# A start-up section rewritten: block 0's masks as their own matmuls, and causal triangles on the tensor engine

## The chip, the core and the metric

One core of a Trainium2 chip runs the whole kernel. Its engines work at once, each from its own queue in order: TensorE (PE, with its weight loads PEld), VectorE (DVE), ScalarE (ACT), GpSimd (POOL, which also issues DMAs) and SyncE (SP, which here only issues DMAs). The metric is the device time of one execution in microseconds. A profile of one execution gives every instruction's start and duration and what ended each wait.

## The reference

Four batches, eight heads, 768 positions of 64 elements. The keys are cut into 24 chunks of 32. Each query takes the six chunks with the largest upper bound of its scores, attends to the causal positions in them, and the result goes through a feed-forward layer with softplus.

```python
k_min, k_max = k_chunks.min(axis=3), k_chunks.max(axis=3)      # per chunk and element
ub = sum(maximum(q * k_min, q * k_max), axis=-1)               # bound per query and chunk
ub = where(causal chunk, ub, -1e9); top = six largest chunks
scores = scale * q @ k.T, where selected and pos_q >= pos_k, else -1e9
attn = softmax(scores) @ v                                     # [4, 8, 768, 64]
x = attn as [3072, 512]
out = softplus(x @ w_in) @ w_out                               # w_in [512, 2048], w_out [2048, 512]
```

## The kernel before

The work is cut into 12 blocks of 256 query positions (three per batch, `NBLK`), and each block into four pairs of heads. A block's way is this.

- Its k and q are loaded and turned so that head elements lie on partitions: blocks 0 to 2 by PE transposes (`kT`, `qT`, L471), later ones by transposing DMAs on SP (L475). k and q of block 0 come as float32 over SP (`load_pairs`, tiles `xp`) and are cast on ACT or DVE (L258, L259); all other loads, the weights too, are issued by POOL (L339, L376, L383).
- DVE reduces k to chunk maxima and minima (`kx`, L490, L498), which are copied into `BD`. The positive and negative parts of q (`qpos`, `qneg`) against `BD` give the bounds (`ub`, L570, L574), from which DVE takes the sixth largest (L597) and writes the mask rows (`mraw`, L612, L615). They are turned (`mT`, L627, L633) and copied into the rows of `qa` and `qt` beside q.
- `ka` and `kb` hold k of a whole batch, one head of each pair in either, and beside it one-hot rows that name each position's chunk. One matmul (L687, L688) over the 96 or 128 rows so yields score and mask at once. The one-hot rows are made by POOL's affine selects in `ohb` (L275 to L279) and spread into `ka` and `kb` by SP (L307).
- ACT takes the exponential of the scores (L695). On the diagonal POOL clears the triangle above it, in place, by an affine select (L705): eight per block, between the exponential and the matmul with v.
- The matmul with v (`av`, L717) carries a column of ones for the sum; DVE divides (L727, L728); the result is turned into `x` (L743 and a copy, or a transposing DMA, L732).
- The feed-forward layer: `h` (L791, 96 tasks of eight matmuls), exp and ln on ACT (L796, L801), `y` (L816), a copy and a store per 128 rows (L827).

The order on every engine is laid out ahead: `make_plan` lists every operation with its engines, its estimated cost, the buffers it takes and a due time from the table `PAR`; `Plan.run` lays them out in time, for each engine the earliest due among those that can start, and the instructions are emitted in that order. `keep_awake` fills PE's planned gaps of the first part with matmuls of a tile of zeros (L852). `PAR` holds the due times (`a`, `prep`, `hlag`, ...), the times of loads (`first`, `loads`, `ahead`) and the number of buffers of each kind (`sizes`).

Of the kernel before, what the change touches and what calls it, by code (L numbers as in the profile page):

```python
# [12 lines left out]
ALU = mybir.AluOpType  # L13
# [50 lines left out]

class Op:
    __slots__ = ("name", "alts", "fn", "deps", "gate", "after", "succ", "alloc", "touch", "key",
                 "rel", "packet", "port", "due", "wait", "eng", "start", "end", "done", "dma", "n", "at", "inst")


class Plan:  # L70
# [5 lines left out]
    def op(self, name, alts, fn, deps=(), alloc=(), touch=(), key=None, dma=None, gate=(), after=(), rel=0.0, packet=19.0, port=False):  # L76
        o = Op()
        o.rel, o.packet, o.port = round(rel), packet, port
# [50 lines left out]
    @staticmethod  # L129
    def home_at(pool, s, e):  # L130
        t = 0.0
        for q, x, dma in pool.ends[s]:
            t = max(t, x + (LANDED[e] if dma else 0 if q == e == "PE" else LAT[q].get(e, 150)))
        return t

    def run(self, par):
# [11 lines left out]
        ring, packet = {"SP": 0.0, "POOL": 0.0}, {"SP": 19.0, "POOL": 32.0}  # L148
# [3 lines left out]
        while ready:  # L152
# [26 lines left out]
            if o.dma:  # L179
                other = "SP" if e == "POOL" else "POOL"  # L180
                at = max(o.end + (650 if e == "SP" else 1150), ring[e], 2650.0)
                back, part = max(0.0, ring[other] - at), packet[other] / o.packet
                ring[e] = at + o.dma + min(o.dma * part, back)
                ring[other] += min(o.dma, back / part)
                packet[e] = o.packet
                o.done = ring[e] + (450 if o.packet < 100 else 1000)
                if e == "SP":
                    o.end = max(o.end, ring[e] - 3500)
            else:
                o.done = o.end  # L190
# [4 lines left out]
            for b in o.touch:  # L195
                b.left -= 1
                b.ends.append((e, o.done, bool(o.dma)))
# [22 lines left out]
def dve(n, rate=1.0):  # L220
    return n / (0.96 * rate) + 66


PAR = dict(
    dmat=3,
    dmaT=450,
    narrow=1,
    l0=1,
    over="soy",
    maskD=3,  # L230
    awake=(1.06, 45.0, 5.7),
    first=(64.42, 64.23, 29.03, 95.39),
    loads=((87.43, 130.15, 71.7), 19.14, (76.86, 12.06, 15.17), 41.22),
    tol={"PE": 0, "ACT": 0, "DVE": 0, "POOL": 2358, "SP": 0},
    alt=636,
    ohd=(229.35, 150.58),
    a=(-46.8, -33.92, -31.03, -0.05, 17.1, 24.77, 54.71, 88.7, 133.12, 175.62, 173.66, 255.42, 297.45, 469.8),
    prep=((77.31, -48.97, -81.43, 46.38), (-8.14, 24.92, -67.86, -43.68), (53.78, -16.07, -58.0, 11.26), (25.03, -41.37, -16.45, 11.23)),
    av=(-0.8, 4.76),
    ot=(12.12, 10.86),  # L240
    hlag=(8.7, 27.7, 34.1, -3.53, 34.9, 33.84, 33.54, 32.2, 25.36, -32.32, 54.03, 77.81),
    ylag=(7.32, 7.87, 25.64, 26.35, 28.67, 47.05, 47.88, 49.45, 10.02, 22.03, 47.36, 37.39),
    ahead=(3.4, 19.67, 10.64, 22.05, 12.72, 9.33, 70.63, 47.4, 103.95),
    sizes=dict(s=2, h=2, y=1, o=1, t=2, xf=2, xp=4, kT=2, io=8, kx=2, q=2, pn=2, ub=2, pt=4, osb=4, x=4, g=2, e=4, ysb=4, mT=2),
# [3 lines left out]
def make_plan(T, par):  # L248
# [19 lines left out]
    P.op("zero", [("DVE", 80)], lambda e: nc.vector.memset(T.zero, 0.0), key=-100000)  # L268
    ident = P.op("ident", [("POOL", 520)], lambda e: make_identity(nc, T.ident), key=1000)
    ohm = P.op("ohm", [("DVE", 700)], lambda e: nc.vector.memset(T.ohb, NEG), key=900)  # L270
    oh = []
    for k in range(NBLK):
        def f(e, k=k):
            x = T.ohb[:, k * QB:(k + 1) * QB]
# [6 lines left out]
        oh.append(P.op("oh", [("POOL", 1330)], f, [ohm], key=1500 + 6000 * k))  # L281
# [13 lines left out]
    chunk_rows = [P.op("c4", [("POOL", 900)], f4, [r4], key=3000)]  # L295
    mr0, bd0, kb0, vone, ohk = [], [], [], [], {}
# [8 lines left out]
    def rows_of(i, k0, k1, h):  # L305
        x = (T.KB[i][32:64] if h else T.KA[i][64:96])[:, :, k0 * QB:k1 * QB]
        return nc.sync.dma_start(out=x, in_=T.ohb[:, k0 * QB:k1 * QB].unsqueeze(1).to_broadcast([32, NP, (k1 - k0) * QB]))  # L307
    for k0, k1 in ((0, 1), (1, NBLK)):
        for h in range(2):
            o = P.op("ohk", [("SP", 450)], lambda e, k0=k0, k1=k1, h=h: rows_of(0, k0, k1, h), oh[k0:k1],  # L310
                     key=par["ohd"][k0] * 1e3, dma=300 * (k1 - k0))
# [16 lines left out]
    def load(nm, n, when, gate=()):  # L328
# [6 lines left out]
        for t in range(NT):  # L335
# [4 lines left out]
                     gate=gate, key=key, rel=key - 2000 if n > 2 else 0.0, dma=950 if n < 3 else 2050, packet=32.0, **new)  # L340
            first = first or o
            ld[nm, n, t] = o

    def load_pairs(nm, n, when):
# [4 lines left out]
        for g in range(2):  # L349
# [4 lines left out]
                     key=1e3 * when[g], dma=950, packet=29.0, alloc=[st])  # L354
# [6 lines left out]
    def load_rows(nm, n, when):  # L361

        for t in range(NT):
            st = Buf(pool["xf"])
            d = P.op(f"ld {nm}{n}.{t}", [("SP", 560)], lambda e, t=t, st=st: nc.sync.dma_start(out=st.ap, in_=rows(nm, n, t)),
                     key=1e3 * (when + 0.3 * t), dma=1000, alloc=[st])
# [5 lines left out]
    def load_w_in(when):  # L372
        for c in range(4):
# [4 lines left out]
            w_in.append(P.op(f"w_in{c}", [("POOL", 800)], f, key=1e3 * (when + 0.4 * c), dma=2550, packet=173.0, after=w_in[-1:]))  # L378

    def load_w_out(when):  # L380
        for c in range(4):
# [4 lines left out]
            w_out.append(P.op(f"w_out{c}", [("POOL", 800)], f, key=1e3 * (when + 0.4 * c), dma=2550, packet=173.0,  # L386
# [5 lines left out]
    load_pairs("k", 0, (0.0, l0[0]))  # L392
    if par["l0"] < 2:
        load_pairs("q", 0, (l0[1], l0[2]))
    else:
        load("q", 0, l0[1])
# [4 lines left out]
    for nm, x in zip("kqv", l1):  # L401
        load(nm, 1, x)
# [545 lines left out]
```

## Time and profile before

| | us |
|---|---|
| Median of 3 runs (264.2 to 266.11) | 266.11 |
| The profiled execution, its own time | 266.59 |
| Its span | 264.8 |
| POOL busy in the span | 110.8 |
| DMA moved | 29.87 MB, mean 113 GB/s |

The span runs from the first to the last instruction of the profile. "Busy" is time in which an engine has an instruction under way. The 40-slice view shows the parts by engine, in tenths:

```profile
PE   8698999999999999999999999999999999999995
DVE  6589961019789667447634596584582164221012
ACT  3589999988687879999687992699997885999900
PEclk9799999999999999999999999999999999999999
```

A slice is 6.6 us. PE counts as busy in nearly all, ACT and DVE in the first third above all; `PEclk` is the granted clock of the tensor engine.

### The profile page before, as it was taken

The page shows a single profiled execution, that of the slowest core. Times are in us where ns is not written, and L with a number is a line of the kernel's source. Part 1 is how long each engine was busy: PE and PEld are TensorE (multiplying, and loading weights), DVE is VectorE, ACT ScalarE, POOL GpSimd, SP SyncE. Part 2 cuts the span into 40 slices and gives each one's busy share as a digit, 9 for nine tenths or more (in the row PEclk, how much of TensorE's full clock was granted, in tenths as well). Part 3 has the DMA queues.
Part 4 walks back from the last instruction along what each step waited for, and adds up shares of the span by engine and source line. Part 5 has one row for each costly group of instructions (what it writes and reads, how often), then busy time and mean ns, then how long its engine had stood idle before and what let it go on. Part 6 is the DMA issues. An engine that isn't in the chain of part 4 may idle for free.

```text
span 264.8 us, 7039 instructions
## 1 busy us (share of the span) xinstructions
PE 255.0 (96%) x2750; PEld 197.2 (74%) x2779; DVE 142.5 (54%) x500; ACT 211.0 (80%) x372; POOL 110.8 (42%) x193
## 2 busy tenths in 40 slices
PE   8698999999999999999999999999999999999995
PEld 8698898768775677788678864777888756887744
DVE  6589961019789667447634596584582164221012
ACT  3589999988687879999687992699997885999900
POOL 8927878798318520543990263401110211310000
PEclk9799999999999999999999999999999999999999
DMA  7996999999999984699699969624440123001022
GB/s 162 161 189 90 181 196 231 155 139 190 149 136 173 132 119 89 115 129 100 73 173 150 117 88 174 173 54 120 45 82 0 42 72 99 10 2 42 0 79 79
DMA packets 114719, 29.87 MB, mean 113 GB/s; under 512 B 104544, under 2 KB 111712, under 8 KB 114688
## 3 DMA queue, kind: packets, MB, share of 16 engines
q0 software_dynamic: 74944, 13.11, 66.5%
q1 hardware_dynamic: 39744, 16.33, 33.0%
q8 instruction: 21, 0.34, 0.6%
q14 instruction: 10, 0.08, 0.1%
HBM read 27.26 MB, written 6.29 MB: 127 GB/s over the span
## 4 chain that ended last, share of the span: by engine, by line
PE 86%; DMA 5%; DVE 3%; ACT 3%; issue 1%; POOL 0%; DVEq 0%; POOLq 0%
PE ph L791 30%; PE py L816 17%; PE pt L816 9%; PE po L717 7%; PE ps L687 5%; PE py L852 4%; PE ps L688 4%; DMA io<-in_k_dram 3%; DMA x<-osb 3%; PE pt L687 2%; PE pt L688 1%; PE pt L570 1%; ACT g L801 1%; PE ph L816 1%; ACT e L796 1%
## 5 line engine op out<-in xcount | busy, mean ns | idle before, releaser
L791 PE MATMUL ph<-x,w_in_sb 128*128 128x256 bf16 x768 | 91.8, 272 | 0.0
L705 POOL TENSOR_SCALAR_AFFINE_SELECT pt<-pt 128x256 bf16<-128x256 bf16 x96 | 39.5, 419 | 112.6 <-ACT pt L695 112.1
L791 PEld LDWEIGHTS <-w_in_sb 128*128 128x128 bf16 x768 | 73.6, 98 | 11.5 <-DMA w_in_sb<-in_moe_w_in_dram 0.5
L695 ACT ACTIVATE pt<-ps 128x512 bf16<-128x512 f32 (+1 forms) x134 | 69.9, 564 | 9.4 <-PE ps L688 8.8
L796 ACT ACTIVATE e<-ph 128x512 f32<-128x512 f32 x96 | 56.3, 606 | 12.5 <-PE ph L791 11.8
L816 PEld LDWEIGHTS <-g 128*128 128x128 bf16 x400 | 37.4, 98 | 31.4 <-ACT g L801 0.5
L816 PE MATMUL py<-w_out_sb,g 128*128 128x512 bf16 x231 | 57.8, 379 | 1.5 <-ACT ysb L258 0.2
L801 ACT ACTIVATE g<-e 128x1024 bf16<-128x1024 f32 x48 | 51.1, 1072 | 1.0
L695 ACT ACTIVATE pt<-pt 128x512 bf16<-128x512 f32 (+1 forms) x58 | 32.4, 584 | 0.6 <-PE pt L688 0.6
L717 PEld LDWEIGHTS <-pt 128*128 128x128 bf16 x672 | 26.8, 97 | 5.1 <-issue 0.6
L259 DVE COPY ysb<-py 128x512 f32<-128x512 f32 x12 | 8.3, 691 | 36.9 <-PE py L816 36.9
L717 PE MATMUL po<-v,pt 128*128 128x65 bf16 x610 | 26.4, 193 | 0.3 <-DVE osb L728 0.3
L816 PE MATMUL pt<-w_out_sb,g 128*128 128x512 bf16 x108 | 26.2, 379 | 0.2
L727 DVE RECIPROCAL rec<-po 128x4 f32<-128x4 f32 x43 | 7.6, 178 | 34.9 <-PE po L717 34.6
L490 DVE TENSOR_REDUCE kx<-kT 128x32 bf16<-128x1024 bf16 x18 | 21.0, 1209 | 8.9 <-DMA kT<-io 8.9
L852 PE MATMUL py<-zero 128*128 128x128 bf16 x243 | 22.7, 245 | 1.1 <-DVE zero L268 1.1
L339 POOL DMA_DIRECT2D v<-in_v_dram x24 | 21.6, 905 | 3.8 <-DMA io<-in_q_dram 1.5
L339 POOL DMA_DIRECT2D io<-in_k_dram x22 | 20.0, 910 | 5.7 <-DMA w_in_sb<-in_moe_w_in_dram 2.2
L339 POOL DMA_DIRECT2D io<-in_q_dram x22 | 19.9, 910 | 0.7 <-PE ph L791 0.6
L728 DVE TENSOR_TENSOR osb<-po,rec 128x256 bf16<-128x256 f32 x43 | 18.2, 424 | 2.7 <-DMA x<-osb 1.3
L852 PEld LDWEIGHTS <-zero 128*128 128x128 bf16 x243 | 18.3, 111 | 1.3 <-DVE zero L268 1.1
L687 PE MATMUL ps<-qa,ka 96*128 96x256 bf16 x71 | 18.3, 273 | 0.7 <-DVE qa L259 0.7
(99 smaller groups left out, 302.5 us busy)
## 6 DMA issues: line engine op xcount, KB each, us to landing
out_dram<-ysb SPq DMA_DIRECT2D x23, 256.0 KB, 2.4
v<-in_v_dram POOLq DMA_DIRECT2D x24, 128.0 KB, 7.6
io<-in_k_dram POOLq DMA_DIRECT2D x22, 128.0 KB, 7.2
io<-in_q_dram POOLq DMA_DIRECT2D x22, 128.0 KB, 7.1
w_out_sb<-in_moe_w_out_dram POOLq DMA_DIRECT2D x4, 512.0 KB, 8.0
w_in_sb<-in_moe_w_in_dram POOLq DMA_DIRECT2D x4, 512.0 KB, 9.6
xp<-in_k_dram SPq DMA_DIRECT2D x2, 256.0 KB, 3.2
xp<-in_q_dram SPq DMA_DIRECT2D x2, 256.0 KB, 6.3
```

The lines of the kernel that those rows point to most:

```text
L339: lambda e, t=t: nc.gpsimd.dma_start(out=into(nm, n, t), in_=rows(nm, n, t)),
L490: nc.vector.tensor_reduce(kx.ap[:, :, j].rearrange("d p (t c) -> d t p c", t=NT), kT.ap.rearrange("d p x -> d (p x)").rearrange("d (t p c ...
L687: nc.tensor.matmul(sp.ap[:, 0:QB], kk[0:nr, p, j * 128:(j + 1) * 128], qq, start=True, stop=True)
L695: lambda e, sp=sp, pt=pt, h=h, j=j, w=w: nc.scalar.activation(pt.ap[:, h, j:j + 2].rearrange("k j c -> k (j c)")[:, 0:w], sp.ap[:, 0:w], A ...
L705: nc.gpsimd.affine_select(out=d, in_=d, compare_op=ALU.is_ge, fill=0.0, base=0, channel_multiplier=-1, pattern=[[0, 2], [1, 128]])
L717: nc.tensor.matmul(o[:, u, h], pt.ap[:, h, j, c0:c0 + 128], T.V[i][:, j, 2 * p + h, :], start=(j == 0), stop=(j == t0 + u))
L728: nc.vector.tensor_tensor(osb.ap[0], o[:, :, :, 0:D], osb.ap[1].to_broadcast([128, NT, 2, D]), op=ALU.mult)
L791: nc.tensor.matmul(o[:, j], T.w_in[:, dt, ft * 128:(ft + 1) * 128], x.ap[:, dt], start=(dt == 0), stop=(dt == KDM - 1))
L796: lambda e, hb=hb, eb=eb, f2=f2: nc.scalar.activation(eb.ap[:, f2 * 512:(f2 + 1) * 512], hb.ap, ACT.Exp),
L801: lambda e, eb=eb, g=g, f4=f4: nc.scalar.activation(g.ap[:, f4 * 4:(f4 + 1) * 4].rearrange("f j c -> f (j c)"), eb.ap, ACT.Ln, bias=1.0),
L816: nc.tensor.matmul(yb.ap[:, 0:c1 - c0], g.ap[:, f, u * 128:(u + 1) * 128], T.w_out[:, f, c0:c1], start=(f == 0), stop=(f == KFF - 1))
L852: z.fn = lambda e: T.nc.tensor.matmul(T.pools["y"].homes[0][:, 0:128], T.zero, T.zero, start=True, stop=True)
```

## The change

Block 0 (`plain = n < 1`) no longer builds `qa` and `qt` rows with masks. Its k is copied once, for both heads of a pair, into a tile `K0`, its transposed masks once into `M0`, and each score is two matmuls into one bank: `K0` with q, and `ohb` with `M0`. For that `ohb` has a second copy of block 0's one-hot columns in partitions 32 to 63 (`ohc`, on DVE or ACT). `ka` and `kb` still get block 0's k, for blocks 1 and 2, by copies from `K0` (`ke`, on POOL or DVE). q is not copied into `qa`.

```diff
+            plain = n < 1
+            if plain:
+                kcs.append(P.op(f"kc{n}", [("ACT", act(L * QB)), ("DVE", ...)],
+                                lambda e, ...: copy(e, *in_turn(T.K0[:, pp], t_of(kT), pairs)), [x0, x1], touch=[kT]))
+                kab[n, gi] = kcs * 2
+                for h in range(2 if ps is groups[-1] else 0):
...
+                        f"ke{n}", [("POOL", 1150), ("DVE", 380)],
+                        lambda e, ...: copy(e, (T.KB if h else T.KA)[i][hs, :, cs], T.K0[hs]),
...
-            qac = P.op(f"qac{n}", ...
+            qac = None if plain else P.op(f"qac{n}", ...
...
+            if plain:
+                mask[n, gi, 0] = mask[n, gi, 1] = P.op(
+                    f"mc{n}", [("DVE", 345), ("ACT", 480)],
+                    lambda e, ...: copy(e, T.M0[:, pp], mT.ap.bitcast(BF16)[0:64, 0:L * QB]...), mt, touch=[mT])
-            for h in range(2):
+            for h in range(0 if plain else 2):
```

In blocks 0 and 1 (`tri = n < 2`) the causal triangle is added to the diagonal's scores by a third matmul, of the identity with a tile `tri` that holds `NEG` above the diagonal; POOL's selects L705 are there for blocks 2 to 11 only.

```diff
+                            parts = [(T.K0, q.ap[1], slice(h * 64, h * 64 + 64)), (T.ohb, T.M0, slice(h * 32, h * 32 + 32))]
+                            for c0, c1, t in ((0, QB, 0), (QB, w, 1)):
+                                for z, (kk, x, ss) in enumerate(parts):
+                                    jj = slice(c0 // 2, c0 // 2 + 128)
+                                    kk = kk[ss, p, jj] if z == 0 else kk[ss, jj]
+                                    nc.tensor.matmul(sp.ap[:, c0:c1], kk, x[ss, p, t * 128:QB], start=z == 0, stop=z == 1 and not tri)
+                                if tri:
+                                    nc.tensor.matmul(sp.ap[:, c0:c0 + 128], T.ident, T.tri, start=False, stop=True)
+                            return
...
-                    if last:
+                    if last and not tri:
                         def f_a(e, pt=pt, h=h, t0=t0):
...
+        tri_ = [P.op("tri", [("POOL", 430)], lambda e: nc.gpsimd.affine_select(
+            out=T.tri, in_=T.tri, compare_op=ALU.is_ge, fill=NEG, base=0, channel_multiplier=-1, pattern=[[1, 128]]), [t0_], key=8000), ident]
```

The one-hot columns are made in their three parts with due times of their own, the first with a due time ahead of the loads; the memset of `ohb` is split likewise. The fillers of `keep_awake` are 512 columns wide where the gap allows, else 128.

```diff
-    ohm = P.op("ohm", [("DVE", 700)], lambda e: nc.vector.memset(T.ohb, NEG), key=900)
+    ohm = [P.op(f"ohm{j}", [("DVE", 270 + 200 * j)], lambda e, j=j: nc.vector.memset(
+        T.ohb[0:32, QB:] if j else T.ohb[0:32, 0:QB], NEG), key=-900000 + 902000 * j) for j in range(2)]
...
-        oh.append(P.op("oh", [("POOL", 1330)], f, [ohm], key=1500 + 6000 * k))
+        oh.append(P.op(f"oh{k}", [("POOL", 1330)], f, [ohm[min(k, 1)]], key=1500 + 6000 * k if k else -900000))
+    ohc = [P.op("ohc", [("DVE", 150), ("ACT", 330)], lambda e: copy(e, T.ohb[32:64, 0:QB], T.ohb[0:32, 0:QB]), oh[:1], port=True, key=9000)]
...
-    fill, free = [], 1e3 * par["awake"][0]
+    fill, free = [], max(1e3 * par["awake"][0], 140 + next(o.end for o in order if o.name == "zero"))
...
+        for w in (512, 128):
```

The planner changes too. A class `Rings` takes the place of two running times for the DMA rings: it shares them out packet by packet between POOL's and SP's queues, and each load has a packet time and a time to land of its own. Due times can be shifted one operation at a time (`tweak`, some 190 entries), and every number of `PAR` is new, so that the whole order is another, in all blocks.

```diff
+        for o in topo:
+            o.due += 1e3 * par["tweak"].get(o.name, 0.0)
...
+    both=0,
+    tri=2,
...
-    tol={"PE": 0, "ACT": 0, "DVE": 0, "POOL": 2358, "SP": 0},
+    tol={"PE": 0, "ACT": 86, "DVE": 192, "POOL": 7510, "SP": 0},
...
-    sizes=dict(s=2, h=2, y=1, o=1, t=2, xf=2, xp=4, kT=2, io=8, kx=2, q=2, pn=2, ub=2, pt=4, osb=4, x=4, g=2, e=4, ysb=4, mT=2),
+    sizes=dict(s=2, h=2, y=1, o=1, t=2, xf=2, xp=4, kT=3, io=5, kx=2, q=3, pn=2, ub=2, pt=3, osb=4, x=5, g=3, e=2, ysb=4, mT=2),
```

`io` are the buffers of k and q, `pt` those of the exponentials, `e` and `g` those between the feed-forward layer's two halves. `both=0` leaves two further functions of the diff (`load_both`, and its transposes) unused.

More of the change, by code (lines that the diff above doesn't have):

```diff
@@ L179, in run @@
             if o.dma:
[L180 to L186, printed above, removed]
+                for x, y in rings.add(o, t - 2500.0):
+                    y += x.land
+                    if x is o or x.done != y:
+                        x.done = y
+                        for z in x.succ:
+                            z.at.clear()
                 if e == "SP":
[L188 removed]
+                    o.end = max(o.end, o.done - o.land - 3500)
             else:
```

257 lines of the change are left out of this document (183 added, 74 removed).

## The prediction

> **What bounds the kernel now.** First the page's engine and filler rows, then the busy time by stage.
>
> ```profile
> span 264.8 us, 7039 instructions
> ...
> PE 255.0 (96%) x2750; PEld 197.2 (74%) x2779; DVE 142.5 (54%) x500; ACT 211.0 (80%) x372; POOL 110.8 (42%) x193
> ...
> L852 PE MATMUL py<-zero 128*128 128x128 bf16 x243 | 22.7, 245 | 1.1 <-DVE zero L268 1.1
> ```
> ```profile
> 0.00:36.06 36.06, 31.54 (x477) 29.30 (x478) 29.20 (x106) 27.53 (x47) 27.38 (x53) 0.95 1.32 159
> 36.06:49.55 13.49, 13.43 (x155) 11.59 (x154) 2.53 (x10) 12.72 (x24) 10.08 (x16) 1.00 1.58 207
> 49.55:261.50 211.95, 210.00 (x2128) 156.33 (x2152) 110.18 (x384) 170.74 (x303) 73.31 (x126) 1.00 0.92 100
> 261.50:264.80 3.30, 0.04 (x1) 0.00 (x0) 0.55 (x2) 0.00 (x0) 0.00 (x0) 1.00 0.23 79
> ```
>
> The columns of a stage are its length, then busy time and count of PE, PEld, DVE, ACT and POOL, then granted clock and DMA. PE looks full, but 22.7 us of it multiply zeros. So I count PE's work by the pace of its stream, with the fillers left out:
>
> ```profile
> 199.94 6.99 PE ph L791 x64
> ...
> 177.92 1.73 PE py L816 x8
> ```
> ```profile
> 20.60 1.56 PE L852 MATMUL py<-zero 128*128 128x128 bf16 x25
> 21.99 0.18 PE L570 MATMUL ph<-bd,qpos 128*128 128x32 bf16 x1
> ...
> 34.15 0.58 PE L717 MATMUL po<-v,pt 128*128 128x65 bf16 x14
> 34.57 0.27 PE L687 MATMUL ps<-qa,ka 96*128 96x256 bf16 x1
> ...
> 36.06 1.03 PE L791 MATMUL ph<-x,w_in_sb 128*128 128x256 bf16 x8
> ```
>
> A matmul of 256 columns takes 6.99/64 = 109 ns, one of 512 takes 216, one of 128 takes 1.39/25 = 56, one of 65 takes 0.42/14 = 30; the smallest are taken at 25. With these the instruction list before adds up to 234.2 us. Of this 11.5 stand ahead of the first feed-forward matmul (L791), which starts at 36.06: 24.6 us are lost there. The rest, 222.7, ends at 261.5, that is 225.4 later: only 2.7 lost in all that follows. 3.3 us close the span, and the execution's 266.59 us hold 1.8 outside it. **So the kernel is a ramp of 36 us, of which two thirds are lost, and then a full PE.** What the change is worth is when that first matmul can start, less any work that it adds behind it.
>
> The Trainium skill ("Trainium Kernel Development and Optimization", Performance Expectations) says that matmul busy time is a bad metric for closeness to a roofline. Here it would leave 264.8 - 255.0 = 9.8 us to gain at most; the count above leaves 27.3, and I go by the count.
>
> **What holds the ramp.** Rows of the timeline, POOL, PE, ACT:
>
> ```profile
> 1.85 1.06 SPq L352 DMA_DIRECT2D xp<-in_q_dram  x2
> 2.08 1.90 POOL L339 DMA_DIRECT2D io<-in_k_dram  x2
> ...
> 9.49 0.45 PEld L471 LDWEIGHTS <-io 128*128 128x128 bf16 x8 [2.41 <-DMA io<-in_k_dram]
> ...
> 10.64 0.62 ACT L258 CAST io<-xp 128x512 bf16<-128x512 f32 x1
> ...
> 13.23 0.59 ACT L258 COPY qt<-pt 128x512 bf16<-128x512 bf16 x1 [0.90 <-PE pt L471]
> ```
> ```profile
> 18.61 1.01 ACT L258 COPY ka<-ph 64x1024 bf16<-64x1024 bf16 x1
> 19.52 0.86 ACT L695 ACTIVATE pt<-ps 128x384 bf16<-128x384 f32 x2
> ...
> 29.13 5.62 ACT L695 ACTIVATE pt<-ps 128x512 bf16<-128x512 f32 x11
> 34.64 0.64 ACT L258 COPY x<-pt 128x256 bf16<-128x256 bf16 x2
> ```
> ```profile
> 8.35 0.52 POOL L275 TENSOR_SCALAR_AFFINE_SELECT ohb<-ohb 32x256 bf16<-32x256 bf16 x1
> ...
> 9.40 0.39 POOL L279 TENSOR_SCALAR_AFFINE_SELECT ohb<-ohb 32x256 bf16<-32x256 bf16 x1
> ...
> 27.55 0.77 POOL L376 DMA_DIRECT2D w_in_sb<-in_moe_w_in_dram  x1
> ...
> 35.43 0.77 POOL L376 DMA_DIRECT2D w_in_sb<-in_moe_w_in_dram  x1 [0.21 <-issue]
> ```
>
> Block 0's q transposes stand on PE behind k's of block 1, which wait for a POOL load until 9.49; its second half is copied only at 13.23. The first exp is at 19.52, block 1's exps start at 29.13, and x of block 0 is complete at 34.64 + 0.64 = 35.3. POOL gives out w_in between the causal selects, from 27.55 to 35.43.
>
> **The change, part by part.** *PE work.* Block 0 computes each score as a 64-row k part and a 32-row mask part: eight more matmuls of 256 columns and eight of 128, 1.3 us. The triangle adds 32 of 128 columns in blocks 0 and 1, 1.8 us. Total 237.3; the two programs happen to have the same 11.5 us ahead of the first L791. That the matmuls with fewer rows are no cheaper I take from the 96-row form above, in step with the rest.
>
> *POOL.* 16 causal selects go. For them and the other steps, the durations:
>
> ```profile
> L705 POOL TENSOR_SCALAR_AFFINE_SELECT pt<-pt 128x256 bf16<-128x256 bf16 x96 | 39.5, 419 | 112.6 <-ACT pt L695 112.1
> ...
> w_in_sb<-in_moe_w_in_dram POOLq DMA_DIRECT2D x4, 512.0 KB, 9.6
> xp<-in_q_dram SPq DMA_DIRECT2D x2, 256.0 KB, 6.3
> ```
> ```profile
> L498 DVE TENSOR_REDUCE kx<-pt 128x16 bf16<-128x512 bf16 x4 | 2.5, 682 | 0.8 <-PE pt L471 0.8
> ...
> L498 DVE TENSOR_REDUCE kx<-pt 128x32 bf16<-128x1024 bf16 x2 | 2.4, 1220 | 0.5 <-PE pt L471 0.5
> ```
> ```profile
> L259 DVE COPY bd<-kx 64x64 bf16<-64x64 bf16 x22 | 5.8, 264 | 0.3
> ...
> L259 DVE COPY qa<-qt 64x1024 bf16<-64x1024 bf16 x11 | 5.5, 497 | 0.0
> ```
> ```profile
> 23.43 0.42 DVE L259 COPY qa<-pt 32x512 bf16<-32x512 bf16 x1
> 23.88 1.36 DVE L597 MAX8 ub<-ph 128x8 f32<-128x12 f32 x16
> 25.16 0.16 DVE L727 RECIPROCAL rec<-po 128x4 f32<-128x4 f32 x1
> 25.36 0.42 DVE L728 TENSOR_TENSOR osb<-po,rec 128x256 bf16<-128x256 f32 x1
> ```
>
> That is 16 x 0.42 = 6.7 us of POOL and, more, the waits on ACT before each. In the new order no select stands among the weight loads; each load waits only until the one eight places ahead of it has landed. POOL's list, with 0.95 for an issue (1.90 for two) and 1.4 for a one-hot triple (8.35 to 9.79), starts its loads at about 2.8 and brings w_in's first issue to about 19.5. Before, 8.5 us from issue to use were enough (27.55 to 36.06), so it is there by 28.0; the median of the four, 9.6, holds later ones that queue behind others, and puts the last at about 32. Block 0's one-hot selects stand, in the built order, behind the loads of block 1, one of w_out, block 2's k and half of v: done at about 12.8. That costs nothing while ACT reaches their copy only at 15.6; the cover is gone once the queue in front of them loses 2.8 us. The same rows go out on SP behind them and, if as slow as POOL's first load (7.4), land at 20.2; only block 1 asks for them, at 24.6. The other half of v is issued at about 13.4 and, after 7.4 as the first load (2.08 to 9.49), lands at 20.8; the av that asks for it comes at 19.7, and 1 us is lost there at worst, on DVE's normalisation, which is free for it only at 20.1.
>
> *The mask of block 0.* POOL's first load goes out some 0.7 later (v's ones and the triangle are ahead of it), which leaves the rings to q's SP loads: the second, issued at about 2.4 and landing some 6.3 to 6.8 later, comes at 8.2 (all of the 0.7 gained, and a little by the head start) to 9.1 (nothing gained); I take 8.2, since k's two came quickly while POOL had not begun. Both casts (0.62) end at 9.4, and PE takes q's transposes without k of block 1 ahead: q is copied by 10.6, where the second half was copied at 13.23 to 13.82. On DVE four half kx end at 8.4. Then four positive and negative parts at about 0.45 (an estimate: under the 0.50 of the copy of 1024) end at 11.9; two bd copies 0.5; one added copy of k, 0.5, behind which stands the bound's maximum; then 0.75 of maxima and mask rows: 13.7. ACT copies them at 14.0 to 14.6, makes block 1's negative q (as the copy of 1024, 1.0) and the second one-hot (as one x copy, 0.32): 15.9, then 0.6 of fillers: scores at 16.6 and exps at 16.9, 2.6 earlier than 19.52.
>
> *DVE sets the rest.* Behind the first mask rows stand, in its order: a k copy 0.5, qa of block 1 0.5, bd 0.5, kx 1.2, the second half's maxima and rows 0.7, kx 1.2, bd 0.5, mask copy 0.42, a PSUM copy of k 0.85 (twice the 0.42 for 512): 6.4, to 20.1. Then four normalisations of 0.6, 1.4 of maxima, 0.5 of mask rows and 0.84 of mask copies: 5.1, to 25.2; then two x copies of 0.3 around a kx of 1.2: 27.0. So x is complete at 27.0 instead of 35.3. The qac copies that are gone and the halved mask copies are already out of this list; all of it is on the path, nothing hides.
>
> *First L791.* PE's order puts it behind block 1's scores, whose bank comes free on ACT: block 1's masks end at 24.6, four exps at 0.51 (5.62/11), one q copy of 1.0 and one more exp give 28.5. I take **28.7**; bounds are 26.5 (no bank wait, the hand-overs as tight as in the rows) and 33 (each of some thirty hand-overs of this chain 0.15 slower).
>
> *Sum.* 28.7 + (237.3 - 11.5) + 2.7 as before + 1.1 = 258.3 for PE, +3.3 = 261.6, +1.8 = 263.4 against 266.59. The shown median is 266.11, so 0.5 lower: **263.0**. The 1.1 is an estimate of what ACT withholds until 55: it reaches its first e at 32.5 (28.5, two k copies of 1.0, four exps), and until then L791 has two banks to fill. Buffers (three pt, two e, five io, where there were four, four, eight) I cost at nothing: e is written and read by ACT alone, in order; the others are a rival.
>
> **The clock.** The trace before has one cold stretch:
>
> ```profile
> 10.00:15.00 5.00, 5.00 (x73) 5.00 (x69) 3.27 (x12) 3.38 (x6) 4.86 (x8) 0.66 2.25 165
> ```
>
> It follows PE's wait that ended at 9.49. The new program has 73 fillers, 40 of them four times as wide, by count 10.5 us instead of 13.6; where a wait outlasts them the clock may fall again, in 16 to 28 too, at up to twice the price of what PE does there, some 2 us at the upper end, none at the lower. I take nothing. The Trainium skill ("TensorE: Matmul & The Clock Gate", Part 1) has the array return to half rate after an idle window of about 3.4 us and stay there until about 3.4 us of activity; by that rule an outlasted filler would cost at most 1.7 us of rate. The trace agrees with the second half only: the row above follows a gap of 2.4 us.
>
> **Rivals.** A change under 1% (2.7 us) is about what a measurement of this kernel cannot tell from none.
>
> *The ramp gives it back* (0.22): DVE is the new bound of the ramp, and if the first L791 comes at 31 to 34, with a cold stretch perhaps, the time is 265.3 to 268.3; 266. For it: the chain has no slack. Against it: DVE and ACT ran above 90% here before too.
>
> *A load holds POOL* (0.18, slower): with five k and q buffers a load waits until a transposing DMA two and a half blocks back has landed, and the selects queued behind it on POOL hold the av matmuls.
>
> ```profile
> kT<-io SPq DMA_TRANSPOSE x9, 8.5
> ```
>
> It decides once a load reaches POOL's head before that transpose lands. At one wait of about 1 us that PE's queue does not cover, in each of nine blocks, the time is 263 + 9 = 272. Against it: from 49.55 on POOL was busy 73.3 of 212 us.
>
> *The order works as laid out* (0.12): no bank waits, first L791 at 25.5 to 26.5: 259 to 260.5.
>
> *The change does less than it says* (in the first rival): the one-hot rows behind loads, above.
>
> **Numbers.** Forecast 261 to 265 with 0.48; of this two thirds lie below 263.4, which is 1% under the median. With the early case: faster 0.44. Same: the last third, 0.16, and the first rival, 0.22: 0.38. Slower: 0.18. Range 259 to 269: it leaves out the slower rival and little else.
>
> **What would show it.** First ACT exp at 16.9 (not 19.5), x complete at 27, first L791 at 28.7, w_in issued by 22; PE 225.8 + about 4 us from there to its end; no select on POOL before block 2. Wrong if the first L791 is later than 31 or if PE loses more than 6 us behind it.

## The result, and the profile after

The changed kernel takes 280.88 us (median of 4 runs, 279.99 to 283.18) against 265.25 for the kernel before beside it: a ratio of 1.0605, 95% interval 1.0521 to 1.0688. It is slower by 6%, where 263.0 and a small gain were forecast. The profiled execution took 280.41 us. Executions of one kernel differ by a per cent or two: the ratios here leave out those more than 1.5% above the shortest of their kernel, the medians do not. The page of the profiled execution, and the busy time by stage, split where the first feed-forward matmul (now L935) starts and where the last matmul ends:

```profile
span 278.5 us, 6797 instructions
...
PE 266.0 (96%) x2657; PEld 192.2 (69%) x2657; DVE 139.3 (50%) x499; ACT 209.5 (75%) x372; POOL 104.9 (38%) x178
```
```profile
0.00:39.27 39.27, 35.39 (x297) 20.84 (x298) 25.63 (x84) 19.47 (x34) 27.57 (x46) 0.83 1.42 182
39.27:275.20 235.93, 230.60 (x2363) 171.37 (x2360) 113.19 (x415) 190.01 (x340) 77.37 (x132) 0.99 0.86 95
```

The ramp is longer than before, 39.27 us against 36.06, and its mean clock is 0.83. Behind it PE takes 235.9 us for work that counts 225.8: 10.1 are lost there, where 2.7 were lost before. Of the 10.1, PE was idle for 5.3 (235.93 - 230.60). Against the kernel before that is 3.2 (ramp) + 3.1 (added work) + 7.4 (later losses) = 13.7 us, the difference of the two spans. Against the forecast it is 10.6 in the ramp (39.27 - 28.7) and 6.3 behind it (10.1 - 3.8).

Where the ramp goes is read from PE's timeline, block 0's scores first, then a score of block 1 and the first feed-forward matmul:

```profile
16.02 0.28 PE L822 MATMUL ps<-qt,k 64*128 64x256 bf16 x1
16.23 0.28 PE L822 MATMUL ps<-m,ohb 32*128 32x256 bf16 x1
16.44 0.23 PE L824 MATMUL ps<-tri,ident 128*128 128x128 bf16 x1
16.60 0.23 PE L822 MATMUL ps<-qt,k 64*128 64x128 bf16 x1
...
36.13 0.27 PE L831 MATMUL ps<-qa,ka 96*128 96x256 bf16 x1
36.24 0.22 PE L833 MATMUL ps<-tri,ident 128*128 128x128 bf16 x1
...
39.27 0.49 PE L935 MATMUL ph<-x,w_in_sb 128*128 128x256 bf16 x3
```

Starts, not durations, tell the pace. In block 0 a matmul of 256 columns holds the stream for 0.21 us and one of 128 for 0.16, where block 1's 96-row matmul of 256 columns, followed by the same triangle, holds it for 0.11. Nothing is waited for between them. And in the middle of this the clock falls. PE alone by window (length, busy time and count, granted clock, DMA share, GB/s):

```profile
15.00:20.00 5.00, 4.99 (x41) 0.94 1.76 163
20.00:25.00 5.00, 5.00 (x54) 0.50 1.54 182
25.00:30.00 5.00, 5.00 (x27) 0.50 1.24 206
30.00:35.00 5.00, 4.64 (x40) 0.70 1.24 206
```

PE is busy all through and runs at half rate from about 19.4 (0.94 is 0.6 us of the first five at half) to about 33 (0.70 is 3 us at half). Block 0's scores last from 16.02 to 29.9 with what stands between them.

### The profile page after: what moved, and what is told of

Its sections match the earlier page's. It is cut to its first block, busy times and chain, and to the rows that moved or that the text cites. A ratio compares the mean times of both kernels' runs of the same rounds, so it can differ in the third digit from the quotient of the medians.

```text
span 278.5 us, 6797 instructions
## 1 busy us (share of the span) xinstructions
PE 266.0 (96%) x2657; PEld 192.2 (69%) x2657; DVE 139.3 (50%) x499; ACT 209.5 (75%) x372; POOL 104.9 (38%) x178
## 4 chain that ended last, share of the span: by engine, by line
PE 78%; DMA 10%; DVE 6%; ACT 1%; SPq 1%; issue 1%; DVEq 0%
PE ph L935 28%; PE py L960 17%; PE ps L831 7%; PE pt L960 6%; PE po L861 5%; DMA x<-osb 5%; PE pt L831 4%; DMA kT<-io 3%; PE ps L822 3%; DMA xp<-in_q_dram 2%; PE pt L693 1%; PE py L997 1%; PE ps L824 1%; PE ph L960 1%; PE pt L861 1%
## 5 line engine op out<-in xcount | busy, mean ns | idle before, releaser
L935 PE MATMUL ph<-x,w_in_sb 128*128 128x256 bf16 x768 | 96.0, 275 | 3.7 <-DMA x<-osb 3.7
L935 PEld LDWEIGHTS <-w_in_sb 128*128 128x128 bf16 x768 | 74.1, 98 | 17.6 <-issue 4.7
L849 POOL TENSOR_SCALAR_AFFINE_SELECT pt<-pt 128x256 bf16<-128x256 bf16 x80 | 32.7, 425 | 130.6 <-ACT pt L839 130.6
L839 ACT ACTIVATE pt<-ps 128x512 bf16<-128x512 f32 (+1 forms) x130 | 68.1, 565 | 16.7 <-PE ps L824 10.4
L960 PE MATMUL py<-w_out_sb,g 128*128 128x512 bf16 x256 | 64.5, 379 | 0.0
L861 PEld LDWEIGHTS <-pt 128*128 128x128 bf16 x672 | 26.5, 98 | 4.4
L960 PE MATMUL pt<-w_out_sb,g 128*128 128x512 bf16 x112 | 26.5, 379 | 0.0
L861 PE MATMUL po<-v,pt 128*128 128x65 bf16 x562 | 24.4, 195 | 0.0
L831 PE MATMUL ps<-qa,ka 96*128 96x256 bf16 (+1 forms) x132 | 22.0, 258 | 0.4 <-DVE qa L333 0.4
L831 PEld LDWEIGHTS <-ka 96*128 96x128 bf16 x184 | 16.6, 98 | 5.2 <-issue 0.8
L831 PE MATMUL ps<-qt,kb 128*128 128x256 bf16 x112 | 19.9, 261 | 0.0
L997 PE MATMUL py<-zero 128*128 128x512 bf16 (+1 forms) x73 | 16.9, 362 | 1.3 <-DVE zero L342 1.3
L872 DVE TENSOR_TENSOR osb<-po,rec 128x256 bf16<-128x256 f32 x39 | 16.6, 425 | 1.4
```

The costliest lines, as they stand in the source:

```text
L831: nc.tensor.matmul(sp.ap[:, c0:c1], kk[0:nr, p, jj * 128:(jj + 1) * 128], x, start=True, stop=not add)
L839: lambda e, sp=sp, pt=pt, h=h, j=j, w=w: nc.scalar.activation(pt.ap[:, h, j:j + 2].rearrange("k j c -> k (j c)")[:, 0:w], sp.ap[:, 0:w], A ...
L849: nc.gpsimd.affine_select(out=d, in_=d, compare_op=ALU.is_ge, fill=0.0, base=0, channel_multiplier=-1, pattern=[[0, 2], [1, 128]])
L861: nc.tensor.matmul(o[:, u, h], pt.ap[:, h, j, c0:c0 + 128], T.V[i][:, j, 2 * p + h, :], start=(j == 0), stop=(j == t0 + u))
L872: nc.vector.tensor_tensor(osb.ap[0], o[:, :, :, 0:D], osb.ap[1].to_broadcast([128, NT, 2, D]), op=ALU.mult)
L935: nc.tensor.matmul(o[:, j], T.w_in[:, dt, ft * 128:(ft + 1) * 128], x.ap[:, dt], start=(dt == 0), stop=(dt == KDM - 1))
```

## The experiments

The theory has two parts. **Height**: a matmul's height is the number of rows of its operands; matmuls of 64, 32 and 128 rows in turn empty the array (the part of TensorE that multiplies) at each change, and this also costs the clock; that is the ramp's share. **Order**: the later losses come from how the new plan orders transfers, and have nothing to do with block 0. The rivals are that ACT, DVE and DMA set the ramp in any case, that the clock falls for another reason, and that the late ramp itself upset the queues behind it.

Ratios are to the kernel before on the same chip. "First" is the start of the first feed-forward matmul and "later loss" what PE takes from there to its end beyond 225.8 us (span less 3.3 less first less 225.8). Span, first and later loss are of the one profiled execution, whose time stands beside the median.

| kernel | ratio (95%) | median | profiled | span | first | later loss |
|---|---|---|---|---|---|---|
| before | 1 | 264.45 to 265.83 | 266.59 | 264.8 | 36.1 | 2.7 (of 222.7) |
| changed | 1.0605 (1.0521 to 1.0688) | 280.88 | 280.41 | 278.5 | 39.3 | 10.1 |
| block 0 over 128 rows, heads summed | 1.0326 (1.0219 to 1.0432) | 274.57 | 273.61 | 271.4 | 30.6 | 11.7 |
| block 0 over 128 rows, zero-padded | 1.0399 (1.0343 to 1.0454) | 275.92 | 276.83 | 274.8 | 30.9 | 14.8 |
| zero-padded, one k transpose earlier | 1.0142 (1.0107 to 1.0176) | 268.75 | 272.24 | 270.4 | 31.9 | 9.4 |
| the same, four v loads later | 1.0065 (1.0026 to 1.0104) | 267.11 | 266.67 | 264.9 | 31.3 | 4.5 |
| changed, only the k transpose earlier | 1.0392 (1.0291 to 1.0493) | 278.33 | 280.06 | 278.2 | 39.3 | 9.8 |

In the fifth row the profiled execution took 3.5 us more than the median, so a part of its later loss is not in the others.

**1. The pace of matmuls by themselves.** Only stretches of matmuls, two of them here:

```
    for z in range(40):
        nc.tensor.matmul(*go(0, 32 if z % 2 else 64, 256), start=True, stop=True)
    full()          # 72 of 128 rows, 256 columns
    for z in range(40):
        nc.tensor.matmul(*go(0, 128 if z % 2 else 64, 256), start=True, stop=True)
```

> Only matmuls, none of the layer: stretches of 256 columns with operands of 64 rows, 64 rows at position 0 and 64 in turn, 64 and 32 rows in turn, 64 and 128 in turn, 96 and 128 in turn, the changed kernel's own sequence of 64, 32 and 128 rows (256 and 128 columns), and 96 rows, with 72 matmuls of 128 rows ahead of each. The theory (a change between 128, 64 and 32 rows empties the array, 96 rows count as 128): about 109 ns a matmul in every stretch of one height and in 96 and 128 in turn; about 213 ns where 64 and 32, or 64 and 128, take turns; in the sequence of three heights about 213 ns at 256 columns and 160 at 128, and a granted clock that falls to about 0.5 some 3 to 4 us into that stretch. Rival one (fewer rows are slow whatever stands beside them): 64 rows alone also take about 213 ns. Rival two (the slow matmuls of the changed kernel waited for operands and not for the array): 109 ns in every stretch and a full clock throughout.

PE's timeline, one row for each stretch: 64 rows; 64 and 32 in turn (L76); 64 and 128 (L79); 96 and 128 (L82); the changed kernel's sequence (L85). Then the granted clock in the three stretches with slow matmuls:

```profile
10.85 4.54 PE L70 MATMUL o<-a,w 64*128 64x256 bf16 x40
...
33.54 10.43 PE L76 MATMUL o<-a,w 64*128 64x256 bf16 x40
...
54.17 8.62 PE L79 MATMUL o<-a,w 64*128 64x256 bf16 x40
...
70.49 4.63 PE L82 MATMUL o<-a,w 96*128 96x256 bf16 x40
...
82.91 16.87 PE L85 MATMUL o<-a,w 64*128 64x256 bf16 x72
```
```profile
38.50:43.90 5.40, 5.40 (x17) 0.50 0.01 3
54.20:62.60 8.40, 8.40 (x41) 1.00 0.00 0
...
87.00:99.50 12.50, 12.50 (x51) 0.50 0.00 0
```

64 rows alone keep step, 4.54/40 = 114 ns, and so do 96 and 128 in turn, 116. With 64 and 128 in turn it is 8.62/40 = 215 at a full clock: a change of height costs some 100 ns. Fewer rows are not slow as such, and there was nothing to wait for: both rivals fall. The Trainium skill ("TensorEngine Tiling (Array Packing)", Tiling Modes, Key Properties) says that changing the tiling mode drains TensorE; the trace shows a cost at each change of height, which agrees, and gives the price. But the clock did not fall where each of 40 matmuls paid this price (64 and 128). So the change alone is not what lowers it.

**2. What the clock follows.**

> Only matmuls, none of the layer, with 72 of 128 rows and 256 columns between the stretches: 150 of 64 rows, 150 of 32 rows, 640 of 128 rows with 16 columns, 100 of 128 and 32 rows in turn. In the first run of matmuls the clock fell where 64 and 32 rows took turns and not where 64 and 128 did. Theory (the clock follows how much of the array works over time, rows x columns for each ns: 300 at 128 rows in step, 135 to 150 with 64 and 128 in turn or with 64 alone, 58 with 64 and 32 in turn): 64 rows alone keep a full clock, 128 and 32 in turn (96) and 32 rows alone (75) lie between the two known cases and tell where the limit is. Rival one (only an array that is emptied all the time loses the clock): 32 rows alone keep the full clock at 109 ns, 128 and 32 in turn lose it. Rival two (32 rows as such): both stretches with 32 rows lose it.

The timeline (64 rows; 32 rows; 128 rows by 16 columns; 128 and 32 in turn) and a window inside each:

```profile
11.89 16.54 PE L70 MATMUL o<-a,w 64*128 64x256 bf16 x150
...
36.33 28.20 PE L73 MATMUL o<-a,w 32*128 32x256 bf16 x150
...
73.97 9.13 PE L76 MATMUL o<-a,w 128*128 128x16 bf16 x347
...
101.24 30.26 PE L79 MATMUL o<-a,w 32*128 32x256 bf16 x100
```
```profile
16.00:20.00 4.00, 4.00 (x39) 1.00 0.00 0
44.00:48.00 4.00, 4.00 (x21) 0.50 0.00 0
80.00:84.00 4.00, 3.72 (x141) 0.50 0.02 4
112.00:116.00 4.00, 4.00 (x14) 0.50 0.00 0
```

Full clock with 64 rows, half with 32 rows alone, with 128 rows by 16 columns, and with 128 and 32 in turn. Rival one falls: a stream of one height, with no change, lost the clock (32 alone). Rival two does not fall so clearly: 16 columns lost the clock without any 32-row matmul, so 32 rows are not needed for it, but both stretches with 32 rows did lose it. Rows x columns for each ns put the cases in order (estimates from the paces above, 300 being 128 rows in step): 149 with 64 alone and 114 with 64 and 128 keep the clock; 96 with 128 and 32 (at 213 ns), 78 with 16 columns, 74 with 32 alone, 65 for the changed kernel's sequence and 58 with 64 and 32 lose it. If this measure is the right one, the limit lies between 96 and 114, about a third of the array at work; without the cases that hold 32 rows it lies between 78 and 114. No run told it more finely, and none shows that the clock follows just this measure. That the clock fell for a reason outside the matmuls is ruled out by experiment 1: the changed kernel's sequence alone brings it to 0.50.

**3. The changed kernel with block 0 at one height.** Same order of instructions; the tiles `M0` and `ohb` get 128 rows, with zeros in the added ones, and the matmuls change so:

```
-  parts = [(T.K0, q.ap[1], slice(h * 64, h * 64 + 64)), (T.ohb, T.M0, slice(h * 32, h * 32 + 32))]
+  parts = [(T.K0, q.ap[1], slice(0, 128)), (T.ohb, T.M0, slice(0, 128))]
```

> The changed kernel in the same order of instructions, with block 0's key and mask matmuls over 128 rows instead of 64 and 32 (mask tiles zero in rows 64 to 127): the scores of block 0 hold both heads of a pair and both heads' masks, so its output isn't the reference's; columns and number of matmuls stay. The theory (the change of height costs some 104 ns a matmul and with it the clock): score matmuls of block 0 at 109 and 56 ns, from 16.5 to about 21 instead of 29.9, granted clock above 0.9 from 20 to 30, first feed-forward matmul between 28 and 31 instead of 39.3, time 268 to 272 if the waits behind the ramp are of the plan's making, 262 to 266 if they came from the late ramp. Rival one (exponentials, evictions and transposes of block 0 set its pace): first feed-forward matmul still later than 36, time 277 to 281. Rival two (the clock falls for another cause than the matmuls' height): 109 ns at first, but a clock of 0.5 from 20 to 30 all the same, first feed-forward matmul at 34 to 36, time 275 to 278.

PE's timeline where block 0's scores begin, and PE by window:

```profile
15.83 0.27 PE L822 MATMUL ps<-qt,k 128*128 128x256 bf16 x1
15.94 0.27 PE L822 MATMUL ps<-m,ohb 128*128 128x256 bf16 x1
```
```profile
20.00:25.00 5.00, 4.49 (x65) 1.00 1.64 173
25.00:30.00 5.00, 4.08 (x51) 1.00 1.24 207
```

The pace is 109 ns, the clock full, and the first feed-forward matmul comes at 30.6, 8.7 us sooner. The span falls by 7.1 us and not by 8.7: the later loss stays, 11.7 us. The time, 274.57, is above the 268 to 272 of the theory; the start of the first feed-forward matmul and the clock are as it has them. So the ramp's share is height and clock, and the later share is not made by the late ramp.

**4. The same with zeros instead of the sum.** k of each head and its one-hot rows get a tile each with zeros in the other rows:

```
+  parts = [(T.K0[h], q.ap[1], slice(0, 128)), (T.oh0[h], T.M0, slice(0, 128))]
...
+  for x in (T.K0[0][64:128], T.K0[1][0:64], T.M0[64:128], T.oh0[0], T.oh0[1]):
+      nc.vector.memset(x, 0.0)
```

> The changed kernel in its own order with block 0's key and mask matmuls over 128 rows, made right by zeros: k of each head in a tile of its own with zeros in the other head's rows, and one-hot rows for each head with zeros elsewhere (one more copy of k for each group of heads and 5 memsets on VectorE; the output is the reference's). The theory: as with both heads summed and a little later, first feed-forward matmul between 30.5 and 32.5, clock above 0.9 throughout the ramp, time 271 to 276. Rival (the summed version gained by what it left out): first feed-forward matmul later than 35, time 278 or more.

275.92 us, first at 30.9: as the theory has it. This is the base of the next two.

**5. One transposing DMA earlier.** In the list of steps as planned, k of block 10 ahead of block 9's masks and a store, both on SyncE's queue:

```
   order = keep_awake(T, order, PAR)
+  for a, n, b in [('kD10', -1, 'mD9')]:
+      xs = [o for o in order if o.name == a]
...
+      order[at:at] = xs
```

> The same with one transposing DMA moved on SyncE's queue: k of block 10 ahead of the masks of block 9 and a store, which it stood behind. The theory (the later losses come from the order on SyncE's queue): k of block 10 is transposed some 4 us earlier, TensorE's loss around 185 to 205 falls from 3.4 us to under 1.7, time 1.5 to 3 us under the zero-padded version. Rival (the transposing DMAs are slow beside the next block's loads wherever they stand): k lands no earlier and the time is within 1 us of the zero-padded version.

SyncE's timeline in the zero-padded kernel, then in the one with the move:

```profile
183.28 1.19 SPq L760 DMA_TRANSPOSE mT<-mraw  x1
...
185.19 1.49 SPq L585 DMA_TRANSPOSE kT<-io  x1
```
```profile
180.40 1.23 SPq L585 DMA_TRANSPOSE kT<-io  x1
...
183.72 1.19 SPq L760 DMA_TRANSPOSE mT<-mraw  x1
```

The chain of waits of the zero-padded kernel (start, length), and its PE by window:

```profile
185.19 11.31 DMA kT<-io
```
```profile
190.00:200.00 10.00, 6.61 (x47) 1.00 1.43 116
```

k stood behind masks that were not yet computed; it then took 11.31 us to land, and PE lost 3.4 us in this window. With k issued at 180.40 PE is busy for 10.00 of the same 10 us (experiment 7 shows the row). The time fell by 7.2 us, to 268.75, more than expected; the profiled executions differ by 4.6, so part of the 7.2 is not placed by a view. That k landed late wherever it stood, the rival, did not come.

**6. The same move alone on the changed kernel**, with `parts` of 64 and 32 rows as the change has them.

> The changed kernel as it is, with the one move on SyncE's queue alone (k of block 10 ahead of block 9's masks and a store), block 0's key and mask matmuls left at 64 and 32 rows. The theory (two independent losses: the ramp's some 8 us from the changing height, and the later ones from the order of transfers): TensorE's loss around 190 to 206 goes, time 3 to 7 us under the changed kernel's 280.9, first feed-forward matmul still at 39. Rival (the move helped only because the repaired ramp ran the queues in another phase): within 1 us of 280.9.

The four executions took 274.90 to 280.06 us. PE by window, in the changed kernel and then with the move:

```profile
200.00:210.00 10.00, 7.63 (x73) 1.00 0.34 72
```
```profile
110.00:120.00 10.00, 7.88 (x89) 1.00 2.30 119
120.00:130.00 10.00, 9.12 (x103) 0.83 1.51 119
...
200.00:210.00 10.00, 10.00 (x96) 1.00 0.43 79
```

The loss of 2.4 us at 200 to 210 is gone with the ramp as late as ever (first feed-forward matmul at 39.3): this wait came from the order on SyncE's queue, not from the ramp. The summed and the zero-padded kernels, whose ramp is repaired, still lose 3.4 us at 190 to 200. But this execution, at 280.06 the longest of the four, lost 3.0 us at 110 to 130 (the changed kernel 0.6), ahead of the move, so its later loss is 9.8. The median, 278.33, is 2.6 us under the changed kernel's, between the theory's 3 and the rival's 1; the ratio, 1.0392, rests on the two shortest executions. What the move is worth by itself is not settled.

**7. Four loads of v later.** On top of experiment 5, and by the same kind of edit, `ld v8.0` and `ld v8.1` go behind the last select of block 5, `ld v9.0` and `ld v9.1` behind selects of block 7.

> The zero-padded version with k of block 10 first, and the loads of v of blocks 8 and 9 (four of the Pool engine's loads) moved behind selects of blocks 5 and 7, since they are not used before their blocks' attention. The theory (transposing DMAs that TensorE waits for, 9.8 us at 104 and 6.5 at 142, are slow beside the loads in flight): both land sooner, TensorE's loss in 100 to 120 and 140 to 150 together falls from 5.0 to under 3.5 us, time 0.5 to 2.5 us under the version with k first. Rival (the order on SyncE's queue alone decides, or the other loads fill the queue all the same): same time within 0.5 us.

The x transpose that PE waited for, in the chain of waits, and PE by window: two fences with k first, then two with v later, and last the same transpose in the zero-padded kernel, which has the loads of v where experiment 5 has them:

```profile
104.38 9.77 DMA x<-osb
```
```profile
110.00:120.00 10.00, 6.87 (x77) 0.83 0.87 87
...
190.00:200.00 10.00, 10.00 (x90) 1.00 0.83 93
```
```profile
102.99 7.46 DMA x<-osb
```
```profile
110.00:120.00 10.00, 9.88 (x117) 1.00 1.13 117
```
```profile
105.50 7.81 DMA x<-osb
```

The transpose lands in 7.46 us instead of 9.77, and PE's losses at 110 to 120 and 140 to 150 together fall from 4.6 to 0.6 us (in the second window it is busy for 8.51 and 9.54). The time is 267.11, 1.6 under the version with k first, and the intervals of the ratios do not overlap: the move gains a little. Where it gains is not shown. The transpose took only 7.81 us in the zero-padded kernel, with all four loads in their old place. And the execution with k first that was profiled is the one of 272.24 us, with a mean clock of 0.994, where the other four have 0.999 to 1.000: its stretch at 110 to 120 (clock 0.83) is not typical of them. The transpose that PE waits for past 140 took 6.5 us before and 6.4 now, and yet PE lost 1.0 less there; why is not shown.

**8. The triangle, laid out anew and in place.** The kernel before with the triangle by matmul, once with its planner laying it out again, once in its own order with the selects taken out of POOL's queue (the edit shown), once so for block 0 alone:

```
+  nc.tensor.matmul(sp.ap[:, 0:128], T.ident, T.tri, start=False, stop=True)
...
+  def f_a(e, pt=pt, h=h, t0=t0, n=n):
+      if n < 2:
+          return None
```

> The kernel before with the causal triangle of blocks 0 and 1 by matmul (32 matmuls of 128 columns instead of 16 selects on the Pool engine) and nothing else of the change, laid out anew by its own planner. The theory: 32 x 56 ns = 1.8 us more work on TensorE, no change of height since 96 rows count as 128: 264 to 268, within 1% of before. Rival (each triangle matmul behind one of 96 rows empties the array): 32 x 104 ns = 3.3 us on top and a lower clock in blocks 0 and 1: 269 to 275.

> The kernel before, in its own order of instructions, with the triangle of blocks 0 and 1 by 32 matmuls of 128 columns and the 16 selects left out of the Pool engine's queue (the output is the reference's). The theory (the triangle itself is cheap, 32 x 56 ns, and the 16.7 us of the kernel with the triangle alone came from its new order): 264 to 268. Rival (the triangle costs by itself, through its matmuls behind 96 rows or through loads that the Pool engine now issues earlier): 272 or more.

> The kernel before, in its own order of instructions, with the triangle by matmul in block 0 alone (8 selects less on the Pool engine ahead of the first feed-forward matmul, 16 matmuls of 128 columns more); block 1 keeps its selects. In place in both blocks the first feed-forward matmul came 1.9 us earlier, for 1.8 us more work. The theory (the selects of block 0 and what stands behind them on the Pool engine set the gain, and each block's matmuls cost 0.9 us): first feed-forward matmul at 34 to 35, time 0.5 to 1.5 us under before. Rival (block 1's selects stand in the way of block 0's and of the loads as much): first feed-forward matmul after 35, time within 0.5 us of before.

Laid out anew: 282.53 us, ratio 1.0666 (1.0590 to 1.0741), outside the theory's and the rival's times. In place: 264.61 us, 0.9992 (0.9970 to 1.0014). The triangle itself costs what it saves: the first feed-forward matmul comes at 34.3 instead of 36.1, for 1.8 us more work. So the 17 us of the first came from its new order, and from behind the ramp, since its first feed-forward matmul came at 34.3 too. PE's waits in the kernel laid out anew (us in total, times, longest):

```profile
PE po L758 <- POOL pt L746: 6.8, 2, 3.6
```

Block 2's selects stood on POOL behind ten loads, issued from 42.69 to 52.71. Selects held by loads are what the forecast's slower rival has, here in another kernel; that the loads waited for a transposing DMA, as it has them, is not shown. For block 0 alone the ratio is 1.0029 (1.0000 to 1.0057): the first feed-forward matmul came even sooner, at 33.9, but PE needed 226.6 us from there to its end instead of 225.4. Neither the theory nor its rival had that.

**9. Block 0's copies put back.** The changed kernel with one matmul of 96 or 128 rows a score again, laid out anew:

> The changed kernel with block 0 as before the change (k copied for each head, q and masks copied, one matmul of 96 or 128 rows a score tile), the triangle by matmul in blocks 0 and 1 and all else of the change kept; the planner lays it out anew. The theory: no clock below 0.9 between 20 and 30, first feed-forward matmul between 30 and 36, time 266 to 272 (the waits behind the ramp, 10.1 against 2.7 us, belong to the new plan and stay). Rival (the ramp is late through the loads' and rows' new order): first feed-forward matmul later than 37, time 277 or more.

281.06 us, ratio 1.0562 (1.0471 to 1.0653): the rival's time without its cause. The first feed-forward matmul is at 32.1 at a full clock, as the theory has it, but it is 242.7 us from there to PE's end, where the kernel before took 225.4. Which of the new order's waits weighs most was not taken apart.

**10. Height in the kernel before.** Its own order, each score matmul of block 0 split into its 64 and 32 rows:

```
+  rows = [slice(64, 128), slice(32, 64)] if h else [slice(0, 64), slice(64, 96)]
```

> The kernel before, in its own order of instructions, with each score matmul of block 0 split into a key part of 64 rows and a mask part of 32 rows from the same tiles (the same sums; 32 matmuls in place of 16). The theory (each change of height empties the array): in block 0 some 213 ns a matmul of 256 columns and 160 of 128, together about 6 us in place of 1.3, first feed-forward matmul at 39 to 43 instead of 36.1, a granted clock that falls below 0.9 somewhere between 19 and 30, time 269 to 275. Rival (TensorE waits for exponentials and evictions in block 0 anyway, so longer matmuls fit in): first feed-forward matmul within 1 us of 36.1, time 264 to 267.

One score in PE's timeline:

```profile
18.71 0.81 PE L694 MATMUL ps<-qt,kb 64*128 64x256 bf16 x4
```

269.69 us, ratio 1.0165 (1.0116 to 1.0215). Four matmuls take some 0.75 us here where two took 0.17. But the first feed-forward matmul comes at 37.5, only 1.4 later, and not at 39 to 43, and no window from 15 to 40 is below full clock. Part of the price went into time in which PE had waited: from 20 to 30 it is busy for 9.94 us, where it was busy for 8.85. The price of a change is confirmed. That the clock stayed full because each score is short, 0.75 us, with full-height work between, fits experiment 2 but is not shown by itself.

## Why the prediction was wrong, point by point

**What bounds the kernel** was right: a ramp, then a full PE, and the time follows when the ramp ends and what is lost behind it. Put back into the forecast's sum, the measured terms give the time: 39.27 + 225.8 + 10.1 + 3.3 + 1.8 = 280.3 (the 10.1 is itself a remainder of the span).

**The mask of block 0 and POOL** came within some 1.3 us of what was worked out: scores at 16.02 (forecast 16.6), first exp at 17.18 (16.9), w_in issued from 18.25 to 21.25 (19.5 to 22), no select on POOL before block 2. From ACT's and DVE's timelines, the first exp and the last x copy of block 0:

```profile
17.18 0.49 ACT L839 ACTIVATE pt<-ps 128x384 bf16<-128x384 f32 x1 [1.98 <-PE ps L824]
```
```profile
36.79 0.28 DVE L333 COPY x<-pt 128x256 bf16<-128x256 bf16 x1
```

x was complete at 37.1 instead of 27.0: ten microseconds were lost after the first exp, and ACT waited for PE ahead of each of block 0's other exps.

**The step that failed first** is PE work: "That the matmuls with fewer rows are no cheaper I take from the 96-row form above, in step with the rest." The row shown had 96 rows; 64 and 32 were costed by it, and the changes between them at nothing. The two-part scores stood in the sum with 1.3 us. In their place 48 matmuls of block 0 (32 parts and 16 triangles) each took some 104 ns more, 5.0 us in all (an estimate from the pace above), and at half clock the columns themselves took twice their time on top (at 24.90 a matmul of 256 columns holds the stream for 0.32 us).

**The second is the clock**: "I take nothing", with 2 us at the upper end. It was looked for behind gaps, and the fillers were counted against gaps. It fell in a stretch without a gap, in which the sequence of scores works the array at about a fifth of its rate (65 of 300). Both together are 8.7 us (experiment 3), which leaves some 3.7 for the clock. The other 1.9 of the ramp's 10.6 lie within the forecast's bounds of 26.5 to 33; which steps they are in was not taken apart.

**The third is the term "2.7 as before + 1.1"**. The 2.7 belonged to the order before and was carried over to an order whose transfers stood elsewhere; 10.1 were lost. That a new order alone can cost as much is shown by the triangle of experiment 8, 1.0666 laid out anew and 0.9992 in place. In the changed kernel 2.4 us of the later loss go with the place of k's transpose on SyncE's queue (experiment 6); which waits hold the rest stays open. Experiments 5 and 7 bring the later loss to 4.5, with four loads and one transpose moved. With height and these moves corrected the terms are 31.3 + 225.8 + 4.5 + 3.3 + 1.8 = 266.7, where the forecast had 263.4. That is the design as meant, and it does not beat the kernel before either (1.0065): 4.8 us of ramp gained, 3.1 paid in work and 1.8 in later waits.

**The rivals.** DVE did not bound the ramp, so the first rival's mechanism did not come. The slower rival had the sign and half the size, and the wrong place: PE waited for no select on POOL; a transpose stood behind masks on SyncE's queue that were not ready. The depth of buffers was weighed, the order on SyncE's queue past the ramp was not, though the forecast had named 6 us behind the first feed-forward matmul as its mark of failure. Every case within the range, which ended at 269, took the pace of PE as known.

No version here beats the kernel before: the triangle in place ties with it.

## What to carry to other kernels

Cost a matmul of another height by the change and not by its columns: here some 100 ns for each change between 128, 64 and 32 rows (96 went with 128 at no price), so group matmuls of one height, or pad with zeros when they are few. A tensor engine that is never idle can still be running at half clock; read the granted clock in the window beside the busy time, above all where matmuls are narrow or low (16 columns, 32 rows). When a planner lays a kernel out anew, the loss behind the ramp is not inherited: read for each queue which transfer stands behind one that cannot start yet. And before a window of one execution is read against another kernel's, see whether its time is near the median.

## What the runs showed of the hardware that was not expected

The clock fell 3 to 5 us into a stretch of low work with PE busy throughout (3.4 us in the changed kernel, 4.2 with 32 rows alone), and came back about as long after full-height work resumed: in the second run of matmuls alone the 32-row stretch ended at 64.5 and the clock was full from about 67.8. The Trainium skill ("TensorE: Matmul & The Clock Gate", Part 1) explains half rate by how busy the engine has been, with an idle window of about 3.4 us; the time scale agrees with these runs, but the engine here was issuing without a gap (10.00 us busy from 20 to 30 in the changed kernel).

Also, 64 rows at positions 0 and 64 in turn, in banks of their own, ran at twice the pace, 40 matmuls of 256 columns in 2.36 us, 59 ns each, in the first run of matmuls alone, where 109 was expected. No kernel here uses it.
